# Storing every split weight tile, and loading the spectra's rows by two transfers of 64 partitions

## The chip, the cores and the metric

The kernel runs on one core of a Trainium2 chip. The metric is the device time of one execution in microseconds. The engines are TensorE (PE; its weight loads are listed apart as PEld), VectorE (DVE), ScalarE (ACT), GpSimd (POOL) and SyncE (SP), which issues most of the DMA transfers. A name with a q, such as SPq, is the queue of instructions by which an engine issues transfers. Each engine works through its own list of instructions in order, so that an instruction that waits holds up all that stand behind it on the same engine.

## The reference

The input `A_u` has 2048 positions of 448 values in float32. Three terms are added: the input, a state-space convolution and a gated block, the last two on the layer-normed input.

```python
x  = A_u                                   # (1, 2048, 448)
xn = layernorm(x)
# the convolution: a kernel of 2048 taps for each of 448 channels
P = exp((A * dt[:, None])[:, :, None] * pos)          # A = -exp(log_A_real) + i A_imag, 256 modes
K = 2 * einsum("dn,dnl->dl", C * dt, P).real
y = irfft(rfft(xn.T, 4096) * rfft(K, 4096))[:, :2048].T + xn * D_skip
# the gated block
h   = sigmoid(xn @ w_gate) * (xn @ w_up)              # (2048, 1792)
out = x + y + h @ w_down
```

`B_x` is not used: both blocks read the normed `A_u`.

## The kernel before, in words

The program is written as two generators, `conv()` and `glu()`, whose pieces are taken in turn according to how far each has come; a planner then places every instruction in its engine's order, with hints (`issue_after`, high priority) from the code. So TensorE's list alternates between matmuls of the gated block and of the convolution.

**The gated block (`glu`).** The 1792 columns of `w_gate` and `w_up` are cut into 14 tiles `f` of 128, in groups of 3, 3, 3, 3 and 2 (`GROUPS`). The positions are done in two halves. In each half every tile is used once: for each of two blocks of 512 positions `gate()` does two chains of eleven matmuls (`gu`, L711), one for each of the two matrices, then the activation and the product; after a group its part of `h @ w_down` is added up (`po`, L836). For precision each weight tile is split into a high part and the rest: `wh`, `wl` for gate and up (128 x 1024 float32 each, 512 KB), `dh`, `dl` for `w_down` (128 x 448, 224 KB each). `wh` and `wl` have two places, `dh` three and `dl` four.

In the first half a tile comes raw (`w_load` into `wraw`, one place; `rd_load` into `rd`), ScalarE makes the high part (L764, L796), VectorE the low part of `w` (L768) and GpSimd that of `d` (L797). The second half takes the groups in the order 2, 3, 4, 1, 0 (`ORDER`). For the nine tiles outside `RAW` the split parts were stored in DRAM in the first half (`wt_d`, `dt_d`, L787), and SyncE loads them (L780, L808). For the five tiles in `RAW`, which are 0, 1, 2, 4 and 5 and so nearly all of the last two groups, the raw tile is loaded a second time, one tile ahead (`coming`) or two (`coming_d`), and GpSimd splits it (L775, L776, L803, L804).

**The convolution (`conv`).** First the parameters are prepared (`prep`) and the first stage of the input's transform is done: 32 rows by 64 columns of positions, a matmul with the constant `wx`, rows stored in `x1_d` (128 rows, one for each real or imaginary part of a frequency in two halves of the columns). Then `kgen` makes the 2048 taps in 56 steps, on all engines, and `first_stage` does the same transform for them and stores rows in `sk_d`. This runs beside the gated block up to about 526 us.

Then `spectra` does the rest in 17 steps: for four frequencies `k` and one half `h` of the channels each (one step has the last frequency alone). `loads(h, k)` fetches the rows of `x1_d` into `sx` and of `sk_d` into `skl` (three places each; 448 KB each) and a table `tb`, three steps ahead; `there()` does the second stage of the transform on both (64 matmuls `pk` and `px`, L923) and evacuates them (ScalarE `oo`, VectorE L929 and L930); `product()` multiplies the spectra (VectorE L936 and L937, GpSimd L939 and L940); `halves()` follows on VectorE (L944, L945); one step later `back()` does the first stage of the inverse (32 matmuls L957 into the same PSUM tiles `pk` and `px`), ScalarE copies the result into `vt` (L963, two places), and SyncE stores it in `v_d` (L971 to L977). Every two steps `turned()` loads rows of `v_d` turned into `vp` (L983), for which SyncE waits until the store has landed. The last stage (`last`, L993) adds to the output.

In `loads` the 128 partitions of `sx` and of `skl` are filled by four transfers of 32 partitions each (`quarters`), since the four blocks of 32 rows lie in another order in DRAM: for `sk_d` the real and imaginary parts of a frequency stand 32 rows apart, and likewise for `x1_d`, where `wx` has 33 cosines first and then 31 sines.

Of the kernel before, what the change touches and what calls it, by code (L numbers as in the profile page):

```python
# [11 lines left out]
F32 = mybir.dt.float32  # L12
# [8 lines left out]
D = 448  # L21
# [23 lines left out]
FCH = [3, 3, 3, 3, 2]  # L45

GROUPS = [list(range(sum(FCH[:i]), sum(FCH[: i + 1]))) for i in range(len(FCH))]
RAW = set(GROUPS[0] + GROUPS[1][1:])
ORDER = [GROUPS, GROUPS[2:] + GROUPS[1::-1]]
DC = 8  # L50
LAG = 3
# [7 lines left out]
def _tables():  # L59

    a = np.arange(NA)[:, None]
    k1 = np.arange(NK1)[None, :]
    ang = 2 * np.pi * ((a * k1) % 64) / 64.0


    wk = np.zeros((4, NA, 2, 2, 32))

    wx = np.zeros((4, NA, 64))
    for j in range(4):
        wk[j, :, 0, j % 2] = np.cos(ang)[:, :32]  # L70
        wk[j, :, 1, j % 2] = -np.sin(ang)[:, :32]
        wk[j, :, 1, j % 2, 0] = np.cos(ang)[:, 32]
        wx[j, :, :NK1] = np.cos(ang)
        wx[j, :, NK1:] = -np.sin(ang)[:, 1:32]
    b = np.arange(NB)[:, None]
    k2 = np.arange(32)[None, :]
    rows = lambda t: t.reshape(32, 2, 32).transpose(1, 0, 2)
    tab = np.zeros((NK1, 2, 2, 32, 2, 32))
    bk = np.zeros((2, 32, 2, 2, 32, 2))
    for q in range(NK1):  # L80
        al = 2 * np.pi * ((b * (q + 64 * k2)) % 4096) / 4096.0
        c, s = rows(np.cos(al)), rows(np.sin(al))
        tab[q, :, 0, :, 0], tab[q, :, 0, :, 1] = c, -s
        tab[q, :, 1, :, 0], tab[q, :, 1, :, 1] = s, c
        if q in (0, 32):
            c, s = c.transpose(2, 0, 1), s.transpose(2, 0, 1)
            bk[q // 32, :, :, 0, :, 0], bk[q // 32, :, :, 0, :, 1] = c, s
            bk[q // 32, :, :, 1, :, 0], bk[q // 32, :, :, 1, :, 1] = -s, c

    tab[0, :, 1] = 0.0  # L90
    tab[32, :, 1] = tab[32, :, 0]
    tab[32, :, 0] = 0.0
    bk = np.tile(bk.reshape(2, 32, 256), (1, 4, 1))
    t32 = np.concatenate([tab[32].reshape(128, 64), bk[1]], 1)
# [34 lines left out]
def s4d_glu_kernel(ctx, tc, io):  # L129
# [326 lines left out]
    def kgen(pk):  # L456
# [127 lines left out]
        for g in range(NCK // NCH):  # L584
            for c in range(NCH):
# [42 lines left out]
                if cn % 4 == 3:  # L628
                    ks = tl["ks"]
                    nc.tensor.matmul(  # L630
                        ko[:, :, 0], ident, dm[:, cn // 4], start=False, stop=True, skip_group_check=True
                    )
                    nc.scalar.copy(ks.rearrange("p s (q b) -> p s q b", q=2), ko.rearrange("p s (b q) -> p s q b", q=2))
                yield WK / 3
                if cn % 4 == 2 and cn > 3 or cn + 1 == NCK:

# [26 lines left out]
    def kept(t, d, f):  # L663
        for i in range(2):
            flat = t[i].rearrange("p i k f -> p (i k f)") if len(t[i].shape) == 4 else t[i]
            yield flat.bitcast(F32), d[i, f]
# [63 lines left out]
        to.append((hh, hl))  # L730

    def glu():
        stores, later, coming, coming_d, rds = [], [], {}, {}, []
        last_fs = [f for fs_ in ORDER[1] for f in fs_]
        follow, second = dict(zip(last_fs, last_fs[1:])), dict(zip(last_fs, last_fs[2:]))
        for half in range(2):
            if half == 1:
                for q in (2, 3):
# [2 lines left out]
            for fs_ in ORDER[half]:  # L741
# [14 lines left out]
                for n_, (f, t) in enumerate(order):  # L756
                    if t == 0:
                        wh = pg.tile([128, 2, 4, 128], F32R, name="wh", bufs=2)
                        if half == 0:
# [8 lines left out]
                                    v.tensor_tensor(wl, raw, wh, ALU.subtract)  # L768
                            if not raws and f + 1 < NFT:
                                raws.append((w_load(f + 1), None))  # L770
                            if f not in RAW:
                                stores.extend(kept((wh, wl), wt_d, f))
                        elif f in RAW:
                            raw, wl = coming.pop(f), w_low()
                            nc.gpsimd.tensor_copy(wh, raw)  # L775
                            nc.gpsimd.tensor_tensor(wl, raw, wh, ALU.subtract)  # L776
                        else:
                            wl = w_low()
                            for t_, d_ in kept((wh, wl), wt_d, f):
                                nc.sync.dma_start(t_, d_)  # L780
                        if half == 1 and follow.get(f) in RAW:
                            coming[follow[f]] = w_load(follow[f])
                        ws.append((wh, wl))
                    between = (lambda s_=mid[n_]: step(*s_)) if cross and mid[n_] else None
                    yield from gate(ws[f - f0], xq[2 * half + t], hs[t], between)
# [4 lines left out]
                    if t == 0:  # L790
                        dh = pg.tile([128, D], F32R, name="dh", bufs=FCH[0])
                        if half == 0:
# [2 lines left out]
                            with hp(HP), tc.issue_after((act if f == 1 else marks)[0].ins):  # L795
                                nc.scalar.copy(dh, rd)  # L796
                            nc.gpsimd.tensor_tensor(dl, rd, dh, ALU.subtract)  # L797
                            if f not in RAW:
                                later.extend(kept((dh, dl), dt_d, f))
                        elif f in RAW:  # L800
                            dl = d_low()
                            rd = coming_d.pop(f)
                            nc.gpsimd.tensor_copy(dh, rd)  # L803
                            nc.gpsimd.tensor_tensor(dl, rd, dh, ALU.subtract)  # L804
                        else:
                            dl = d_low()
                            for t_, d_ in kept((dh, dl), dt_d, f):
                                nc.sync.dma_start(t_, d_)  # L808
                        if half == 1 and second.get(f) in RAW:
                            if len(rds) < 2:  # L810
                                tag, n = (("rdw", 1), ("rd", RB))[len(rds)]
                                rds.append(pg.tile([128, D], F32, name="rd", tag=tag, bufs=n))
                            else:
                                rds.append(rds.pop(0))
                            coming_d[second[f]] = rd_load(second[f], rds[-1])
                        wts.append((dh, dl))
                    yield 2.5
                    for s_ in end[n_] if cross else ():
# [41 lines left out]
    def spectra(pf):  # L860
# [8 lines left out]

        vp = {0: pf.tile([128, 32, H], F32, name="vp", bufs=1)}  # L870
        spare = {
            "vt": [pf.tile([128, 4, H], F32, name="vt", bufs=2)],
            "oo": [pf.tile([128, 2, H], F32, name="oo", bufs=2)],
            "kk": [pf.tile([128, 2, 2, H], F32, name="kk", bufs=1)],
        }
# [4 lines left out]
        def loads(h, k):  # L880
            sx = pf.tile([128, 4, H], F32, name="sx", bufs=NLD)
            sk = pf.tile([128, 7, 4, 32], F32, name="skl", bufs=NLD)
            turn_ = lambda r: slice(*{0: (0, 32), 32: (64, 96), 64: (32, 64), 96: (96, 128)}[r])
            quarters = [(32 * r, slice(32 * r, 32 * r + 32)) for r in (0, 2, 1, 3)]
            if k == 32:
                for r, s in quarters:
                    nc.sync.dma_start(sx[s, 0:2].rearrange("b h d -> b (h d)"), x1_d[r])
                for i in range(2):
                    for r, s in quarters:
                        nc.sync.dma_start(sk[s, :, i], sk_d[i, 0, turn_(r), :, :32])  # L890
                return None, sk, sx
            ds = slice(H * h, H * h + H)
            for r, s in quarters:
                nc.sync.dma_start(sx[s], x1_d[r + k : r + k + 4, :, ds].rearrange("k b d -> b k d"))
            if k not in tabs:
                tabs[k] = pf.tile([128, 4, 64], F32, name="tb", bufs=NTB)
                nc.sync.dma_start(tabs[k], io["c_tab"][k // 4])
            tb = tabs.pop(k) if h else tabs[k]

            for r, s in quarters:  # L900
                nc.sync.dma_start(sk[s].rearrange("p g k d -> p g (k d)"), sk_d[h, k // 4, turn_(r)])
            return tb, sk, sx

        def after():
# [41 lines left out]
            return sd  # L946

        def back(h, k, sd, engs=(nc.sync, nc.sync)):
            vt = work("vt", [128, 4, H], 2)
            n = 2 if k == 32 else 4  # L950
            bt = t32[:, 1:].rearrange("p (q e) m -> p q e m", q=2) if k == 32 else bk
            with after():
# [53 lines left out]
                out_end(ac[:, 4 * q - 8 : 4 * q - 4], 4 * q - 8, ds, [nc.sync])  # L1006

        ac = acl[0]
        lasts.append(last)
        nc.sync.dma_start(t32, io["c_t32"])  # L1010
        nc.gpsimd.dma_start(bk, io["c_bk"])
# [195 lines left out]
```

## The time and the profile before

| | us |
|---|---|
| median of three runs (745.04 to 748.52) | 745.27 |
| the profiled execution | 745.18 |
| its span, first to last instruction | 743.4 |
| TensorE busy | 666.0 (90%) |
| VectorE busy | 588.1 (79%) |
| ScalarE busy | 421.1 (57%) |
| GpSimd busy | 389.4 (52%) |
| mean granted TensorE clock | 0.955 |
| moved by DMA | 114.47 MB, 154 GB/s |

A busy share is a mean over stages that are limited by different things, so the stages have to be read apart. Rows of the profile give the line in the code (L711), the engine, the operation and the tiles, written as output<-input. In rows of a timeline the first number is the start, the second the duration; in brackets stands how long the engine had been idle before, and what ended that. Rows of waits read: who waited, for whom, total time, how many times, the longest. Rows by tile give the shortest, median and longest duration in ns. In windows the pairs are busy time and number of instructions; the last three columns are the granted clock, the share of time in which the 16 DMA engines were busy, and GB/s. The "chain" is the sequence of work that ended last, each piece with its duration.

### The profile page before, as it was taken

Reading aid. Unit: us, or ns where it says so; the run is one execution under the profiler, and the core shown is the slowest. Engines: PE = TensorE matmul, PEld = TensorE weight load, DVE = VectorE, ACT = ScalarE, POOL = GpSimd, SP = SyncE. Lnnn points to the kernel's source line nnn. Section 1 sums busy time; section 2 is a strip of 40 time slices with the busy share of each in tenths; the row PEclk is TensorE's granted clock in tenths of the full one; section 3 lists DMA queues with packets and bytes.
Section 4 is the critical chain, followed back from the end, with each engine's and each line's share of the span. In section 5 each row is a group of like instructions: output and inputs, shape, how many; then the busy total and the mean of one; then the engine's idle time right before and its main releaser. Section 6 shows DMA issues by size and latency. Waiting matters only on the chain.

```text
span 743.4 us, 20855 instructions
## 1 busy us (share of the span) xinstructions
PE 666.0 (90%) x8581; PEld 515.0 (69%) x8581; DVE 588.1 (79%) x779; ACT 421.1 (57%) x651; POOL 389.4 (52%) x415
## 2 busy tenths in 40 slices
PE   2898999998999998989999999999899888589895
PEld 1665788887877885558778878888666565356673
DVE  5799996798998998884789988879387865276753
ACT  3655572887788788973877787686223212122310
POOL 2120044987999887783357758674255433251301
PEclk9999999999999999988999999999999988779997
DMA  8935347355154553439522432331577577776355
GB/s 199 239 110 195 116 146 230 135 158 170 56 155 143 165 163 123 157 125 269 144 92 81 134 132 69 108 94 59 163 194 243 159 203 196 225 214 172 100 166 158
DMA packets 99311, 114.47 MB, mean 154 GB/s; under 512 B 13696, under 2 KB 90048, under 8 KB 98960
## 3 DMA queue, kind: packets, MB, share of 16 engines
q1 hardware_dynamic: 79664, 97.00, 44.3%
q10 hardware_dynamic: 18816, 14.57, 6.7%
q0 software_dynamic: 736, 1.56, 0.8%
q8 instruction: 68, 1.11, 0.6%
q14 instruction: 27, 0.22, 0.1%
HBM read 68.32 MB, written 44.76 MB: 152 GB/s over the span
## 4 chain that ended last, share of the span: by engine, by line
PE 33%; DVE 9%; DMA 8%; ACT 3%; issue 3%; SPq 3%; POOL 2%; ACTq 0%; DVEq 0%; POOLq 0%
PE gu L711 13%; PE po L836 6%; PE ko L620 3%; DMA skl<-sk_d 3%; DMA v_d<-vt 2%; DVE Ft L606 2%; PE tr L536 2%; PE pk L923 2%; DVE Et L604 1%; PE pk L957 1%; PE px L957 1%; PE kp L562 1%; DVE Et L605 1%; DMA acc_d<-acc 1%; PE px L923 1%
## 5 line engine op out<-in xcount | busy, mean ns | idle before, releaser
L514 POOL TENSOR_TENSOR me<-me,pm 128x32 f32<-128x32 f32 (+1 forms) x168 | 141.9, 845 | 91.5 <-DVE Et L605 78.3
L514 POOL TENSOR_TENSOR mf<-mf,pm 128x64 f32<-128x64 f32 (+1 forms) x112 | 119.2, 1064 | 6.0
L711 PE MATMUL gu<-xh,wh 128*128 128x512 f32 x336 | 103.4, 415 | 2.7 <-ACT xh L218 1.4
L711 PE MATMUL gu<-xh,wl 128*128 128x512 f32 x336 | 97.8, 398 | 0.0
L711 PE MATMUL gu<-xl,wh 128*128 128x512 f32 x336 | 96.5, 393 | 0.0
L605 DVE TENSOR_TENSOR Et<-me,S 128x1024 f32<-128x1024 f32 x56 | 80.3, 1434 | 12.1 <-ACT me L527 12.1
L606 DVE TENSOR_TENSOR Ft<-mf,S 128x1024 f32<-128x1024 f32 x56 | 83.2, 1485 | 8.0 <-PE ko L620 5.2
L836 PE MATMUL po<-dh,hh 128*128 128x448 f32 (+1 forms) x227 | 87.6, 386 | 1.2 <-ACT hh L727 0.9
L604 DVE TENSOR_TENSOR Et<-me,S 128x1024 f32<-128x1024 f32 x56 | 79.7, 1423 | 9.1 <-ACT S L547 8.9
L836 PE MATMUL po<-dl,hh 128*128 128x448 f32 (+1 forms) x227 | 85.1, 375 | 1.9 <-POOL dl L797 1.9
L836 PE MATMUL po<-dh,hl 128*128 128x448 f32 (+1 forms) x227 | 84.8, 374 | 2.1 <-DVE hl L729 2.1
L711 PEld LDWEIGHTS gu<-xh,wh 128*128 128x128 f32 x336 | 62.6, 194 | 24.7 <-issue 8.8
L727 ACT CAST hh<-gu 128x512 fp32r<-128x512 f32 x56 | 33.2, 593 | 81.9 <-DVE gu L722 80.0
L544 ACT ACTIVATE S<-tr 128x1024 f32<-128x1024 f32 x56 | 57.8, 1032 | 31.5 <-PE tr L536 29.8
L711 PEld LDWEIGHTS gu<-xh,wl 128*128 128x128 f32 x336 | 64.3, 192 | 15.6 <-issue 0.7
L711 PEld LDWEIGHTS gu<-xl,wh 128*128 128x128 f32 x336 | 63.8, 190 | 14.3 <-issue 0.7
L939 POOL TENSOR_TENSOR yy<-yy 128x448 f32<-128x448 f32 (+1 forms) x16 | 28.6, 1786 | 76.4 <-DVE yy L936 76.4
L620 PEld LDWEIGHTS ko<-Et,Ft 128*32 128x32 f32 x3584 | 53.4, 110 | 21.4 <-issue 10.5
L841 DVE SCALAR_TENSOR_TENSOR acc<-po,acc 128x448 f32<-128x448 f32 (+1 forms) x81 | 48.5, 609 | 23.1 <-PE po L836 23.0
L620 PE MATMUL ko<-Et,Ft 128*32 128x64 f32 x3584 | 63.1, 221 | 3.9 <-DVE Ft L606 3.9
L547 ACT ACTIVATE S<-S,hpi 128x1024 f32<-128x1024 f32 x56 | 65.7, 1173 | 0.0
L545 ACT ACTIVATE S<-tr 128x1024 f32<-128x1024 f32 x56 | 57.7, 1030 | 0.8 <-issue 0.8
(208 smaller groups left out, 1301.1 us busy)
## 6 DMA issues: line engine op xcount, KB each, us to landing
sk_d<-sk ACTq DMA_DIRECT2D x14, 512.0 KB
sx<-x_d SPq DMA_DIRECT2D x64, 112.0 KB
skl<-sk_d SPq DMA_DIRECT2D x64, 112.0 KB
vp<-v_d SPq DMA_DIRECT2D x8, 896.0 KB
v_d<-vt SPq DMA_DIRECT2D x27, 224.0 KB
wt_d<-wh SPq DMA_DIRECT2D x9, 512.0 KB
wt_d<-wl SPq DMA_DIRECT2D x9, 512.0 KB
wl<-wt_d SPq DMA_DIRECT2D x9, 512.0 KB
```

The source lines that it names most:

```text
L514: ins = nc.gpsimd.tensor_tensor(m[:, :, w + a : 2 * w : n], m[:, :, a:w:n], par(base + i).unsqueeze(2).to_broadcast([128, 4 * DC, w // n]) ...
L544: nc.scalar.activation(rows(cs), pv, AF.Abs)
L545: nc.scalar.activation(rows(S[:, 0:5:4]), pv, AF.Sin, scale=TWO_PI)
L547: sins[:] = [nc.scalar.activation(cs, cs, AF.Sin, scale=-TWO_PI, bias=hpi)]
L604: v.tensor_tensor(Et[:, :, :, 32:64], two(me[:, :, 32:64]), S[:, 1::-1], ALU.mult)
L605: v.tensor_tensor(Et[:, :, :, 0:32], two(me[:, :, 0:32]), S[:, 1:3, :, ::-1], ALU.mult)
L606: fts[:] = [v.tensor_tensor(Ft, two(mf), S[:, 3:5], ALU.mult)]
L620: nc.tensor.matmul(ko[32 * j : 32 * j + 32, sl], Ft[:, cc, DC * h + 4 * q + j], Et[:, cc, DC * h + 4 * q + j], start=(k == 0), stop=(k == ...
L711: glu_mm[:] = [nc.tensor.matmul(ps, a_, b_, start=(n == 0), stop=(n == len(mm) - 1))]
L727: nc.scalar.copy(hh, hf)
L836: glu_mm[:] = [nc.tensor.matmul(po[:, ds], a_[:, bs], w_[:, ds], start=(n == 0), stop=(n == 3 * fc - 1))]
L841: v.scalar_tensor_tensor(acc[:, b, ds], po[:, ds], 0.5, acc[:, b, ds], ALU.mult, ALU.add)
```

## The change

Three things change together.

1. `RAW` is gone: the split parts of all 14 tiles are stored in the first half and loaded in the second. The second loads of raw tiles (`coming`, `coming_d`, `rds`) and GpSimd's second splits (L775, L776, L803, L804) go.
2. The tables and one copy put the real and imaginary parts of a frequency in neighbouring rows (`wx`: cosines in even columns, sines in odd ones; `ks` is no longer reordered, so that the rows of `sk_d` come out interleaved). With that, `loads` fills `sx` and `skl` by two transfers of 64 partitions in place of four of 32.
3. `vt` gets a third place, in the memory of `wraw`, and the three are taken in turn.

```diff
-RAW = set(GROUPS[0] + GROUPS[1][1:])
...
-        wx[j, :, :NK1] = np.cos(ang)
-        wx[j, :, NK1:] = -np.sin(ang)[:, 1:32]
+        wx[j, :, 0::2] = np.cos(ang)[:, :32]
+        wx[j, :, 1::2] = -np.sin(ang)[:, :32]
+        wx[j, :, 1] = np.cos(ang)[:, 32]
...
-                    nc.scalar.copy(ks.rearrange("p s (q b) -> p s q b", q=2), ko.rearrange("p s (b q) -> p s q b", q=2))
+                    nc.scalar.copy(ks, ko)
...
-                            if f not in RAW:
-                                stores.extend(kept((wh, wl), wt_d, f))
-                        elif f in RAW:
-                            raw, wl = coming.pop(f), w_low()
-                            nc.gpsimd.tensor_copy(wh, raw)
-                            nc.gpsimd.tensor_tensor(wl, raw, wh, ALU.subtract)
+                            stores.extend(kept((wh, wl), wt_d, f))
                         else:
                             wl = w_low()
                             for t_, d_ in kept((wh, wl), wt_d, f):
                                 nc.sync.dma_start(t_, d_)
-                        if half == 1 and follow.get(f) in RAW:
-                            coming[follow[f]] = w_load(follow[f])
...
-                            if f not in RAW:
-                                later.extend(kept((dh, dl), dt_d, f))
-                        elif f in RAW:
-                            dl = d_low()
-                            rd = coming_d.pop(f)
-                            nc.gpsimd.tensor_copy(dh, rd)
-                            nc.gpsimd.tensor_tensor(dl, rd, dh, ALU.subtract)
+                            later.extend(kept((dh, dl), dt_d, f))
...
-            "vt": [pf.tile([128, 4, H], F32, name="vt", bufs=2)],
...
-            quarters = [(32 * r, slice(32 * r, 32 * r + 32)) for r in (0, 2, 1, 3)]
+            halves_ = [slice(64 * q, 64 * q + 64) for q in range(2)]
...
-            for r, s in quarters:
-                nc.sync.dma_start(sx[s], x1_d[r + k : r + k + 4, :, ds].rearrange("k b d -> b k d"))
+            for q, s in enumerate(halves_):
+                rows = x1_d[64 * q + 2 * k : 64 * q + 2 * k + 8, :, ds]
+                nc.sync.dma_start(sx[s], rows.rearrange("(k c) b d -> (c b) k d", c=2))
...
-            for r, s in quarters:
-                nc.sync.dma_start(sk[s].rearrange("p g k d -> p g (k d)"), sk_d[h, k // 4, turn_(r)])
+            for q, s in enumerate(halves_):
+                nc.sync.dma_start(sk[s].rearrange("p g k d -> p g (k d)"), sk_d[h, k // 4, q::2])
...
-            vt = work("vt", [128, 4, H], 2)
+            vts.append(vts.pop(0))
+            vt = vts[-1]
...
+        vts = [pf.tile([128, 4, H], F32, name="vt", bufs=2) for _ in range(2)]
+        vts.append(pg.tile([128, 4, H], F32, name="vt", tag="wraw", bufs=1))
```

More of the change, by code (lines that the diff above doesn't have):

```diff
@@ L732, in glu @@
     def glu():
-        stores, later, coming, coming_d, rds = [], [], {}, {}, []
-        last_fs = [f for fs_ in ORDER[1] for f in fs_]
-        follow, second = dict(zip(last_fs, last_fs[1:])), dict(zip(last_fs, last_fs[2:]))
+        stores, later = [], []
         for half in range(2):
@@ L808, in glu @@
                                 nc.sync.dma_start(t_, d_)
[L809 to L815, printed above, removed]
                         wts.append((dh, dl))
@@ L882, in loads @@
             sk = pf.tile([128, 7, 4, 32], F32, name="skl", bufs=NLD)
-            turn_ = lambda r: slice(*{0: (0, 32), 32: (64, 96), 64: (32, 64), 96: (96, 128)}[r])
-            quarters = [(32 * r, slice(32 * r, 32 * r + 32)) for r in (0, 2, 1, 3)]
+            halves_ = [slice(64 * q, 64 * q + 64) for q in range(2)]
             if k == 32:
-                for r, s in quarters:
-                    nc.sync.dma_start(sx[s, 0:2].rearrange("b h d -> b (h d)"), x1_d[r])
+                for q, s in enumerate(halves_):
+                    to = sx[s, 0:2].rearrange("b h d -> b (h d)")
+                    nc.sync.dma_start(to, x1_d[64 * q : 64 * q + 2].rearrange("c b d -> (c b) d"))
                 for i in range(2):
-                    for r, s in quarters:
-                        nc.sync.dma_start(sk[s, :, i], sk_d[i, 0, turn_(r), :, :32])
+                    for q, s in enumerate(halves_):
+                        nc.sync.dma_start(sk[s, :, i], sk_d[i, 0, q::2, :, :32])
                 return None, sk, sx
             ds = slice(H * h, H * h + H)
-            for r, s in quarters:
-                nc.sync.dma_start(sx[s], x1_d[r + k : r + k + 4, :, ds].rearrange("k b d -> b k d"))
+            for q, s in enumerate(halves_):
+                rows = x1_d[64 * q + 2 * k : 64 * q + 2 * k + 8, :, ds]
+                nc.sync.dma_start(sx[s], rows.rearrange("(k c) b d -> (c b) k d", c=2))
             if k not in tabs:
@@ L898, in loads @@
             tb = tabs.pop(k) if h else tabs[k]
-            for r, s in quarters:
-                nc.sync.dma_start(sk[s].rearrange("p g k d -> p g (k d)"), sk_d[h, k // 4, turn_(r)])
+            for q, s in enumerate(halves_):
+                nc.sync.dma_start(sk[s].rearrange("p g k d -> p g (k d)"), sk_d[h, k // 4, q::2])
             return tb, sk, sx
```

## The prediction

> **What bounds the kernel now.** I read the page's slices first, then busy time by stretches, then TensorE's waits in the worst stretch, then the queue or engine behind each wait. The slices (about 18.6 us each) show the granted TensorE clock, the share of the DMA engines and the bytes per time:
>
> ```profile
> PEclk9999999999999999988999999999999988779997
> DMA  8935347355154553439522432331577577776355
> GB/s 199 239 110 195 116 146 230 135 158 170 56 155 143 165 163 123 157 125 269 144 92 81 134 132 69 108 94 59 163 194 243 159 203 196 225 214 172 100 166 158
> ```
>
> The clock sags at the end, where DMA is steadily at 0.7. The stretches, with each engine's busy time, clock, DMA share and GB/s:
>
> ```profile
> core 0 of [0], span 743.4 us
> core 0: us, PE busy (x) PEld busy (x) DVE busy (x) ACT busy (x) POOL busy (x), PEclk, DMA share, GB/s
> 0.00:60.00 60.00, 43.84 (x206) 31.62 (x210) 48.01 (x112) 28.46 (x44) 10.59 (x25) 0.97 0.76 189
> 350.00:526.00 176.00, 172.44 (x2773) 142.45 (x2772) 148.39 (x154) 131.77 (x188) 113.36 (x133) 1.00 0.34 103
> 566.00:665.00 99.00, 75.27 (x1025) 53.88 (x1017) 62.07 (x88) 21.71 (x43) 41.70 (x31) 0.84 0.74 212
> 665.00:685.00 20.00, 19.58 (x270) 13.89 (x255) 13.94 (x22) 4.89 (x9) 5.43 (x4) 1.00 0.64 167
> 685.00:713.00 28.00, 24.82 (x365) 17.17 (x363) 21.47 (x34) 8.45 (x17) 6.24 (x4) 0.88 0.35 100
> ```
>
> From 350 to 526 TensorE is the bound: 172.4 of 176 us busy, clock 1.00. From 566 to 665, where the spectral steps meet the last split weights, it stands 99.0 - 75.3 = 23.7 us, and what it does runs at 0.84. If the slow clock falls on busy and idle time alike, its work at full clock is 75.3 x 0.84 = 63.2 us (estimate), so 12.0 us are slow clock: 99 = 63.2 + 12.0 + 23.7. This stage is what the change is worth. Its waits on TensorE (total, times, longest):
>
> ```profile
> PE pk L957 <- DVE kk L930: 13.4, 4, 10.5
> PE pk L923 <- ACT vt L963: 6.6, 3, 2.9
> PE pk L923 <- DMA skl<-sk_d: 3.6, 1, 3.6
> ```
>
> **The change part by part.**
>
> *No weight is split twice.* Out go, for tiles 0, 1, 2, 4, 5 in the second half, a raw load into `wraw`/`rd` and four GpSimd instructions. GpSimd's time is worth nothing by itself (41.7 of 99 us busy), but its order is. The long wait, on GpSimd's timeline:
>
> ```profile
> 623.26 2.04 POOL L939 TENSOR_TENSOR yy<-yy 128x448 f32<-128x448 f32 x1 [2.10 <-DVE yy L936]
> 642.59 0.56 POOL L803 CAST dh<-rd 128x448 fp32r<-128x448 f32 x1 [17.29 <-DMA rd<-in_B_w_down_dram]
> 643.11 1.12 POOL L940 TENSOR_TENSOR yy<-xx 128x448 f32<-128x448 f32 x1
> 644.19 1.13 POOL L804 TENSOR_TENSOR dl<-rd,dh 128x448 fp32r<-128x448 f32 x1
> ```
>
> L940 of a spectral step stands 17.3 us behind a cast for the last `po` group, which waits for a late `rd`. VectorE's L944 waits for L940, everything on VectorE stands behind it, and L957 waits 10.5 us. Without the cast L940 follows L939 at 625.3. What is late next is VectorE's ordinary evacuation, which costs in a calm step:
>
> ```profile
> 688.41 0.99 PE L957 MATMUL pk<-xx,bk 32*64 32x224 f32 x16 [1.22 <-DVE kk L930]
> ```
>
> So 10.5 becomes 1.2: **-9.3**.
>
> *The third place for `vt`.* The 6.6 us are the next step's matmuls waiting for PSUM, whose copy into `vt` waits for the store of two steps before:
>
> ```profile
> ACT vt L963 <- DMA v_d<-vt: 24.9, 5, 7.6
> ```
>
> With three places the copy looks at a store one step (some 10 us) older, more than the longest of these waits, 7.6. **-6.6**. The third place has no user left by then (by the diff `wraw` is loaded in the first half only, and `x1`, which shares it, is stored with the first half's last group).
>
> *Transfers of 64 partitions.* SyncE's queue over two steps of the stage:
>
> ```profile
> 588.41 1.30 SPq L977 DMA_DIRECT2D v_d<-vt  x2
> 592.32 0.50 SPq L983 DMA_DIRECT2D vp<-v_d  x1
> 592.92 1.95 SPq L901 DMA_DIRECT2D skl<-sk_d  x4
> 594.98 2.89 SPq L894 DMA_DIRECT2D sx<-x_d  x4
> 599.01 1.24 SPq L977 DMA_DIRECT2D v_d<-vt  x2
> 600.35 2.42 SPq L901 DMA_DIRECT2D skl<-sk_d  x4
> 602.87 1.79 SPq L894 DMA_DIRECT2D sx<-x_d  x4
> 604.76 0.39 SPq L646 DMA_DIRECT2D wraw<-in_B_w_gate_dram  x1
> 605.20 1.80 SPq L648 DMA_DIRECT2D wraw<-in_B_w_gate_dram  x2
> 607.04 0.59 SPq L646 DMA_DIRECT2D wraw<-in_B_w_up_dram  x1
> 607.67 1.13 SPq L648 DMA_DIRECT2D wraw<-in_B_w_up_dram  x2
> 608.91 0.62 SPq L977 DMA_DIRECT2D v_d<-vt  x1
> ```
>
> It is never free: 20.5 us a round (588.41 to 608.91), against 63.2/99 x 20.5 = 13.1 us of TensorE's work. So loads go out late. Afterwards: `v_d` 1.30, the wait for its landing 2.6, `vp` 0.5, two `skl` 1.0, two `sx` 1.2 (bound from above by two `v_d` stores, also 64 partitions of four short rows), a wait as before 599.01 of 1.1, `v_d` 1.24, `skl` 1.0, `sx` 1.2, and in place of 4.1 us of raw loads two issues like this one:
>
> ```profile
> L780 SPq DMA_DIRECT2D wh<-wt_d x9: 337/338/387, 298.2 to 493.0; - x9
> ```
>
> Together 11.9 us, below 13.1. If 64 partitions take as long to issue as two of 32, only the raw loads go: 20.5 - 3.4 = 17.1. The 3.6 us wait for `skl` goes in the first case and stays in the second, and its landing is unchanged either way; I take half: **-1.8**.
>
> *The clock.* Idle left is 23.7 - 9.3 - 6.6 - 1.8 = 6.0. Short gaps cost clock too: in 685 to 713, 3.2 us idle go with 24.8 x 0.12 = 3.0 us of slow clock, about one for one. The gate of eleven matmuls behind the 1.22 us gap above, and a later one, in the chain:
>
> ```profile
> 690.46 4.31 PE gu L711 x11
> ...
> 696.44 2.72 PE gu L711 x11
> ```
>
> So 6.0 of the 12.0 stays: **-6.0** (ends: 0, and -9.0 if the loss shrinks in proportion to the idle time). [...]
>
> *More bytes.* In this stage two raw `w` loads of 736 KB become pairs of 1024 KB and one `rd` load of 224 KB becomes up to three pairs of 448 KB: +1.7 MB on 212 x 99 = 21.0 MB. What is left by the terms so far is 99 - 23.7 = 75.3 us. If the DMA engines were never free they would need 22.7 MB / (212/0.74 = 286 GB/s) = 79.4 us, and at the best slice's 269 GB/s 84.4. So 4 to 9 us come back; output and `ac` transfers may slip past 665, where the share is 0.64 and 0.35, so I stay near the lower end: **+5.0**.
>
> *Five more tiles stored in the first half*, 4 issues and 1472 KB each, on SyncE, the `dt` pair behind GpSimd's `dl`:
>
> ```profile
> SPq L787 <- POOL dl L797: 38.9, 8, 8.5
> ```
>
> Five more such waits would be 5 x 4.9 = 24 us of SyncE's time, with `ph` and the next raw tile queued behind; TensorE is covered by a raw tile's lead over its gate. Where the lead is thin is the start: tiles 0 and 1 add 3.0 MB to the first 60 us, 12 us of the DMA engines at 189/0.76 = 249 GB/s, and 0.24 x 60 = 14.4 us are free. Bounds 0 (bytes are only added, so no gain) and 12; the nearest wait is ACT's for a raw tile:
>
> ```profile
> 53.22 1.05 ACT L764 CAST wh<-wraw 128x1024 fp32r<-128x1024 f32 x1 [1.49 <-DMA wraw<-in_B_w_up_dram]
> ```
>
> I take **+1.5**.
>
> *At nothing:* the `ks` copy moves the same 512 elements per partition, fourteen times; TensorE's work up to 526 hides it, and even 1 us more of each would cost at most 14 us bare. The tables are constants. After 665 the last stores and loads keep their lengths: 0, plus or minus 2.
>
> **Sum:** -9.3 - 6.6 - 1.8 - 6.0 + 5.0 + 1.5 = -17.2. The profiled execution took 745.18 (1.8 around its span), 0.1 below the median: 745.2 - 17.2 = **728.0**.
>
> **The rivals.**
>
> *All of it comes back.* Transfers slip freely past 665, the first stage absorbs its stores, `skl` is never late, the clock loss shrinks in proportion: -9.3 - 6.6 - 3.6 - 9.0 = -28.5, 716.7. For it: the DMA share of 0.35 after 685. Against: the share of 0.74 before.
>
> *Only GpSimd's stall goes.* `v_d`'s landing, not the place, holds the steps: -9.3, clock in proportion 12.0 x 9.3/23.7 = -4.7, +5.0 + 1.5: 737.7. For it: SyncE's own order, store, landing, `vp`, `skl`, stays serial.
>
> *The transfers set the pace, no change.* If the best slice wholly inside the stage, 225 GB/s, is what rows this short give, 22.7 MB take 100.9 us against 99 now: 745.2 + 1.9 + 1.5 = 748.6 at most, 746 if some slip past 665. For it, one load's landing, three times the issue of its four parts:
>
> ```profile
> 592.92 6.02 DMA skl<-sk_d
> ```
>
> [...] Against the rival: 269 GB/s in one slice.
>
> *Slower: SyncE stands behind a weight load.* The split pair goes straight into `wh`/`wl`, so SyncE must wait until the gates of the tile two before are over; raw loads waited for `wraw` only. Now:
>
> ```profile
> SPq L780 <- PE gu L711: 10.2, 9, 4.0
> ```
>
> That was harmless while SyncE had little else. Here `sx` and `skl` stand behind. A stop ordered before loads that TensorE needs next costs issue and landing, 1.0 + 6.0, and clock at 12.0/23.7 of it, 3.5: 10.5 us. Four tiles load here; four stops: +42 - 23.7 + 1.5 = 765. Against: each load has a whole tile of gates as lead. It decides from the second stop on (17.2/10.5 = 1.6).
>
> **How the numbers follow.** Forecast 0.45, all of it 0.17, only the stall 0.14, transfers 0.13, slower 0.11. A measurement can tell about 0.5%, 3.7 us, from no change. Faster: 0.45 + 0.17 + 0.14 = 0.76; same 0.13; slower 0.11. The range 713 to 745 takes in the first three and a part of the fourth, and leaves out the slower case, the rest of the fourth and a tail below.
>
> **What would show it.** Right: no L775, L776, L803, L804 on GpSimd; the 10.5 us wait at L957 and ACT's waits for `v_d` gone; steps (L923 to L923) of about 8 us instead of some 10 between 566 and 665; SyncE idle at times there; a DMA share near 0.9; clock above 0.9. Wrong: TensorE waiting for `skl` or `sx` with a weight load just ahead on SyncE, or an order of the planner's that shifts work in the first half.

## The result, and the profile after

| | before | after |
|---|---|---|
| median of eight runs each, us | 746.14 | 741.62 (738.91 to 743.78) |
| ratio, with its 95% interval | | 0.9933 [0.9907, 0.9959] |
| span of the profiled execution, us | 743.4 | 742.0 |
| moved by DMA, MB | 114.47 | 125.76 |
| GpSimd busy, us | 389.4 | 350.7 |

The change gains 4.5 us where 17.2 were forecast. 741.6 lies inside the range, near its upper end. The slices of the page of the changed kernel, 18.6 us each, to be held against those of before:

```profile
PEclk9899999999999899787899999999999899969989
DMA  8986558444244453433854243233389987889356
GB/s 202 261 264 248 172 178 275 152 158 149 74 126 166 140 134 102 151 121 109 244 144 138 64 132 95 75 113 95 110 199 294 255 242 205 256 215 284 113 154 171
```

In slices 33 to 36 (595 to 668 us) the clock read 8, 8, 7, 7; now it reads 9, 9, 9, 6, with DMA at 8, 7, 8, 8 where it was at 7 in all four. But in slices 17 to 20 (297 to 371 us), where it read 9, 8, 8, 9, a deeper sag stands now: 7, 8, 7, 8. The windows of the changed kernel (columns as in the prediction):

```profile
0.00:60.00 60.00, 41.59 (x185) 30.43 (x186) 46.21 (x109) 27.43 (x43) 10.49 (x25) 0.94 0.91 245
60.00:170.00 110.00, 106.69 (x735) 85.23 (x734) 99.58 (x146) 68.14 (x109) 50.58 (x58) 0.98 0.59 194
170.00:290.00 120.00, 113.46 (x1725) 92.58 (x1724) 109.54 (x113) 93.86 (x135) 96.98 (x98) 0.96 0.39 123
290.00:350.00 60.00, 52.20 (x678) 31.19 (x676) 44.49 (x55) 46.87 (x77) 32.16 (x44) 0.83 0.39 123
350.00:526.00 176.00, 174.30 (x2650) 143.08 (x2651) 144.88 (x152) 128.73 (x186) 108.94 (x133) 0.98 0.42 127
566.00:665.00 99.00, 81.25 (x1184) 58.08 (x1184) 70.43 (x104) 26.72 (x51) 32.78 (x22) 0.89 0.89 246
```

and the same stretches of the kernel before that the prediction did not show:

```profile
60.00:170.00 110.00, 104.06 (x727) 84.34 (x723) 99.39 (x149) 71.87 (x115) 53.07 (x59) 1.00 0.51 162
170.00:290.00 120.00, 115.50 (x1862) 92.93 (x1864) 111.86 (x117) 97.39 (x143) 105.66 (x103) 0.99 0.43 130
290.00:350.00 60.00, 53.93 (x711) 36.85 (x706) 46.39 (x57) 42.45 (x69) 36.83 (x46) 0.91 0.61 189
```

Between 566 and 665 us TensorE does 1184 matmuls in place of 1025: the stage gains. From 170 to 526 us it does fewer, 5053 against 5346, at a lower clock: something is lost there, where the change was thought to touch nothing. Where it is lost is seen when the start of the same `po` group of the gated block is compared in the two traces. In the changed kernel it stands later by 2.9 us at 114 us (time of the kernel before), 9.5 at 241, 13.5 at 312, 14.6 at 461; then it catches up: later by 6.2 at 612, earlier by 0.1 at 723. So **14.6 us are lost before the spectral steps and 14.7 are won back in them**.

The stage looks as forecast in most points. A spectral step (start of `pk` to the next) takes 8.2 us (ten steps, 561.64 to 643.98) where it took 10.2 (seven, 565.50 to 636.72), each up to the longest wait of the stage. TensorE's waits in it, changed kernel:

```profile
PE pk L972 <- DMA vp<-v_d: 9.9, 1, 9.9
PE pk L936 <- DVE kk L908: 3.6, 3, 1.3
PE gu L711 <- DMA wh<-wt_d: 3.0, 1, 3.0
PE pk L901 <- ACT vt L942: 1.0, 2, 0.5
```

The 10.5 us behind GpSimd are gone (L936 is the old L957; 1.3 is the longest now), and TensorE's wait for `vt` falls from 6.6 to 1.0. ScalarE's own waits for `v_d`, which were to go, fall from 24.9 to 6.2 us. But a wait of 9.9 us for `vp` is new. SyncE's list there, and the end of the wait on TensorE:

```profile
643.90 1.67 SPq L956 DMA_DIRECT2D v_d<-vt  x2
646.23 1.13 SPq L879 DMA_DIRECT2D skl<-sk_d  x2
647.46 1.26 SPq L872 DMA_DIRECT2D sx<-x_d  x2
648.76 0.61 SPq L875 DMA_DIRECT2D tb<-in_c_tab_dram  x1
649.47 1.25 SPq L956 DMA_DIRECT2D v_d<-vt  x2
655.76 0.50 SPq L962 DMA_DIRECT2D vp<-v_d  x1
661.65 1.78 PE L972 MATMUL pk<-vp,wf 64*32 64x224 f32 x32 [9.89 <-DMA vp<-v_d]
```

The load of `vp` waits for the store issued at 649.47, and both stand in line on SyncE: the copy for that store was over at 634.28, 15.2 us ahead of it. Here the third place let ScalarE copy earlier, but the store waited for its turn on SyncE.

What is slow in the middle shows on TensorE itself. The same operations, first in the changed kernel, then in the kernel before:

```profile
298.94 1.50 PE L283 MATMUL gu<-xt,wx 32*64 32x448 f32 x4 [1.48 <-DVE xr L222]
300.47 1.93 PE L620 MATMUL ko<-Et,Ft 128*32 128x64 f32 x64
302.33 1.22 PE L536 MATMUL tr<-sel,ph 128*128 128x512 f32 x2
305.17 1.65 PE L711 MATMUL gu<-xh,wh 128*128 128x512 f32 x3
```

```profile
300.63 0.97 PE L283 MATMUL gu<-xt,wx 32*64 32x448 f32 x4
301.86 1.10 PE L620 MATMUL ko<-Et,Ft 128*32 128x64 f32 x64
303.14 0.71 PE L536 MATMUL tr<-sel,ph 128*128 128x512 f32 x2
306.28 0.93 PE L711 MATMUL gu<-xh,wh 128*128 128x512 f32 x3 [1.11 <-DVE xr L222]
```

The changed kernel takes 1.93 us where 1.10 was enough, for some 10 us on end, and 1.48 us is the longest wait in the 40 us ahead of it. So the loss is largely slow clock: counted as the prediction did, length times (1 - clock) over the five stretches up to 526 us, it is 24.3 us after and 8.4 before, 15.9 more, about the 14.3 by which the `po` group at 515 us is late.

### The profile page after: what moved, and what is told of

It reads as the page before. It is cut to its first block, busy times and chain, and to the rows that moved or that the text cites. A ratio compares the mean times of both kernels' runs of the same rounds, so it can differ in the third digit from the quotient of the medians.

```text
span 742.0 us, 20710 instructions
## 1 busy us (share of the span) xinstructions
PE 671.6 (91%) x8581; PEld 515.9 (70%) x8581; DVE 584.2 (79%) x779; ACT 421.6 (57%) x651; POOL 350.7 (47%) x395
## 2 busy tenths in 40 slices
DMA packets 97630, 125.76 MB, mean 169 GB/s; under 512 B 12656, under 2 KB 85808, under 8 KB 97280
## 4 chain that ended last, share of the span: by engine, by line
PE 54%; DVE 14%; DMA 10%; ACT 6%; POOL 6%; issue 5%; SPq 3%; ACTq 0%; DVEq 0%; POOLq 0%
PE gu L711 20%; PE po L814 15%; PE ko L620 5%; PE tr L536 3%; POOL me L514 3%; DVE Ft L606 3%; DVE Et L605 2%; DVE Et L604 2%; PE gu L283 2%; PE pk L936 2%; DMA vp<-v_d 2%; POOL mf L514 2%; DMA wh<-wt_d 1%; PE pk L901 1%; DMA v_d<-vt 1%
## 5 line engine op out<-in xcount | busy, mean ns | idle before, releaser
L514 POOL TENSOR_TENSOR me<-me,pm 128x32 f32<-128x32 f32 (+1 forms) x168 | 134.4, 800 | 107.0 <-DVE Et L605 94.7
L711 PE MATMUL gu<-xh,wh 128*128 128x512 f32 x336 | 105.8, 422 | 7.5 <-ACT xh L218 4.5
L605 DVE TENSOR_TENSOR Et<-me,S 128x1024 f32<-128x1024 f32 x56 | 74.9, 1337 | 20.0 <-ACT me L527 15.7
L604 DVE TENSOR_TENSOR Et<-me,S 128x1024 f32<-128x1024 f32 x56 | 79.8, 1424 | 9.5 <-ACT S L547 9.5
L544 ACT ACTIVATE S<-tr 128x1024 f32<-128x1024 f32 x56 | 57.9, 1034 | 30.3 <-PE tr L536 23.7
L620 PEld LDWEIGHTS ko<-Et,Ft 128*32 128x32 f32 x3584 | 55.1, 113 | 24.1 <-issue 9.7
L620 PE MATMUL ko<-Et,Ft 128*32 128x64 f32 x3584 | 64.7, 225 | 5.9 <-DVE Ft L606 5.6
L719 ACT ACTIVATE th<-gu 128x512 f32<-128x512 f32 x56 | 34.0, 607 | 43.4 <-PE gu L711 43.4
```

Of the source, the lines that this page charges most:

```text
L514: ins = nc.gpsimd.tensor_tensor(m[:, :, w + a : 2 * w : n], m[:, :, a:w:n], par(base + i).unsqueeze(2).to_broadcast([128, 4 * DC, w // n]) ...
L544: nc.scalar.activation(rows(cs), pv, AF.Abs)
L604: v.tensor_tensor(Et[:, :, :, 32:64], two(me[:, :, 32:64]), S[:, 1::-1], ALU.mult)
L605: v.tensor_tensor(Et[:, :, :, 0:32], two(me[:, :, 0:32]), S[:, 1:3, :, ::-1], ALU.mult)
L620: nc.tensor.matmul(ko[32 * j : 32 * j + 32, sl], Ft[:, cc, DC * h + 4 * q + j], Et[:, cc, DC * h + 4 * q + j], start=(k == 0), stop=(k == ...
L711: glu_mm[:] = [nc.tensor.matmul(ps, a_, b_, start=(n == 0), stop=(n == len(mm) - 1))]
```

## The experiments

The planner writes TensorE's list. Of its 5345 instructions 866 stand at another place in the changed kernel than before, all from the 476th to the 2993rd: the middle of the run. Leaving parts of the change out shows which part does that: the two stores of `dh` and `dl` of **tile 5 alone**. Without them 18 instructions differ. So theory A: the new order costs the 11 to 14 us. Theory B: the traffic of the five added tiles costs them. Theory C: another part of the change does.

### The stores of single tiles

**no5**, **no012** and **nostore** don't store tile 5, tiles 0 to 2, or all five, and so compute another output; **bstore** is the kernel before that stores all 14 but loads as before. Core of the edits (`nostore` has all five tiles in the list; the second half then loads other tiles' parts):

```diff
-                            stores.extend(kept((wh, wl), wt_d, f))
+                            if f not in (5,):
+                                stores.extend(kept((wh, wl), wt_d, f))
```

> The changed kernel without the stores of tile 5 (the second half reads tile 10's parts in its place, so the output is another). Without these four stores the planner puts TensorE's list up to 526 us back to that of the kernel before in all but 18 of 5345 places. Theory A (the planner's order of the first half costs about 11 of the 14 us that the changed kernel lies behind at the start of the spectra): 731, lag against the kernel before about 3 us at 350 us of the span. Theory B (the stores' traffic costs it): only a fifth of the traffic goes, 739, lag still 12.

> The changed kernel without the stores of tiles 0, 1 and 2 (the second half reads tiles 6, 7, 8 in their place, so the output is another); TensorE's list is that of the changed kernel in every place. Theory A (order): only what the first 60 us lose comes back, 3.5 us: 738. Theory B (traffic): three fifths of the stored bytes and all of them in the crowded start go, 8 to 11 us come back: 731 to 734.

> The changed kernel without the stores of tiles 0, 1, 2, 4 and 5 (the second half reads tiles 6 to 10 in their place, so the output is another); TensorE's list is that of the kernel before in all but 18 places. Theories A and B alike: the lag before the spectra goes, 728. If instead the tables, the plain copy of ks or the new second half cost the first half its time (theory C): about 741.

> The kernel before with all 14 tiles stored and nothing else changed; TensorE's list up to the end is that of the changed kernel. Theories A and B: the kernel before plus 14 us less what its own stall hides, 757 to 760. Theory C (the stores and the order they bring cost nothing, the lag comes from the rest of the change): 746.

Then the smallest part, and two versions of the whole change that keep the old order nearly: **no5d** leaves out the two `dt` stores of tile 5, and so computes another output; **d5pool** issues these two from GpSimd's queue (65 instructions from the order before); **d5late** issues tile 5's four stores two gates later (215).

```diff
-                            later.extend(kept((dh, dl), dt_d, f))
+                            later.extend((t_, d_, nc.gpsimd if f in (5,) else nc.sync) for t_, d_ in kept((dh, dl), dt_d, f))
```

> The changed kernel without the two 224 KB stores of tile 5's dh and dl (the second half reads tile 10's in their place, so the output is another); all other stores are there. The planner's TensorE list goes back to that of the kernel before but for 18 places. Theory A (order): 728, as without all of tile 5's stores; lag against the kernel before under 3 us at 460 us of the span. Theory B (traffic): half a megabyte in 742 us of transfers, no change, 741.

> The changed kernel, complete, with those same two stores issued by GpSimd instead of SyncE. The bytes are all there; TensorE's list differs from that of the kernel before in 65 of 5345 places, from the changed kernel's in 897. Theory A: 728 to 731. If the two stores cost time by being made at all: 741.

> The changed kernel, complete, with all four stores of tile 5 issued by SyncE two gates later. TensorE's list differs from that of the kernel before in 215 places, from the changed kernel's in 830. Theory A, if what counts is being near the old list: 728 to 733. If any departure from the old list costs, or the stores themselves: 738 to 742.

### The three parts apart

The second question is which part gains in the spectra. **vt2**, **quart** and **part1** are the changed kernel without the third place, with four transfers of 32 partitions, and with both (stored tiles alone); all three have the changed kernel's order on TensorE. **halves** is the kernel before with two transfers of 64 alone, and its order.

```diff
-        vts.append(pg.tile([128, 4, H], F32, name="vt", tag="wraw", bufs=1))
```

> The changed kernel without the third place for vt (everything else as in it; TensorE's list of instructions is the changed kernel's). Theory F (the prediction's term): the matmuls' wait for the copy into vt comes back, 6.6 us, and with it its share of the clock's term, 6.0 x 6.6/17.7 = 2.2: 741.6 + 8.8 = 750.4, and the trace shows ACT waiting for v_d<-vt again in the spectral steps. Theory G (SyncE's order holds the steps: v_d's store is issued some 15 us after the copy into vt, so that a place one step older is not what is late): within 2 us of the changed kernel, 740 to 744.

> The changed kernel with x and kernels loaded by four transfers of 32 partitions, with the tables and the copy into ks of the kernel before (TensorE's list is the changed kernel's). Theory F (the prediction's term): the wait for skl comes back, 1.8 us taken, 3.6 whole, with 0.6 to 1.2 of clock: 744 to 746.4. Theory G (SyncE's queue still sets the pace of the spectral steps in the changed kernel): a round of it grows by the prediction's 17.1 - 11.9 = 5.2 us, over the three or four steps in which TensorE waits behind it: +15 to +21, 757 to 763, with longer waits for vp, sx or skl on TensorE between 566 and 665 us.

> The changed kernel's stored tiles alone: x and kernels by four transfers of 32 partitions and two places for vt, as in the kernel before (TensorE's list is the changed kernel's). Theory F: the sum of the two terms, 741.6 + 8.8 + 2.4 = 753, of which the first half's loss of 14.5 stays and the spectra gain GpSimd's 9.3 less what the bytes take back. Theory G: as with quarters alone, 757 to 763, the place for vt adding nothing.

> The kernel before with x and kernels loaded by two transfers of 64 partitions, with their tables and the copy into ks; nothing else (TensorE's list is that of the kernel before). Theory F: -1.8 (0 to -3.6) and some clock: 0.994 to 1.0 of the kernel before, about 743.5 beside 745.2. Theory G (SyncE's queue sets the pace): a round of 20.5 us loses 2.0 + 1.6 or so of issue in each of six steps, but the raw loads and GpSimd's 10.5 us stay, so that between a third and all of it shows: -6 to -18, ratio 0.976 to 0.992.

The same three edits on **d5pool**, whose middle is calm:

> The changed kernel with tile 5's two dt stores issued by GpSimd, and without the third place for vt. Theory F (the prediction's term): 726.3 + 6.6 + 2.2 = 735. Theory G (SyncE's queue was what made v_d's stores late; with halves the place is not the limit): within 3 us of d5pool, 723 to 729, ratio to the kernel before 0.970 to 0.977.

> The changed kernel with tile 5's two dt stores issued by GpSimd, and x and kernels by four transfers of 32 partitions as before. Theory F: 726.3 + 2 to 5 = 728 to 731. Theory G: as much as the changed kernel lost by it, 750.05 - 741.6 = 8.4, to the 13 that halves alone gave: 735 to 739, with TensorE waiting for skl or vp in the spectra.

> The changed kernel with tile 5's two dt stores issued by GpSimd, but with four transfers of 32 partitions and two places for vt: stored tiles alone, in the calm order. Theory F: GpSimd's 9.3 and its clock less what the bytes take back: 745.2 - 9.3 - 4.7 + 5.0 = 736. Theory G: what stored tiles alone gained in the spectra in the disturbed order, 7.4, or a little less, since SyncE's queue takes the rest: 737 to 741, and within 3 us of d5_quart (the third place adds nothing there either).

### All results

"Middle" is how much later or earlier the `po` group at 461 us stands than the one at 114, each against the kernel before; "spectra" the same from 461 to 723; both from the profiled execution. The ratios are to runs of the kernel before that were timed beside each kernel, whose medians lie between 744.6 and 746.8 us.

| kernel | TensorE's order | median, us | ratio to before, 95% interval | middle | spectra |
|---|---|---|---|---|---|
| after | new | 741.6 | 0.9933 [0.9907, 0.9959] | +11.7 | -14.7 |
| bstore | new | 761.1 | 1.0189 [1.0141, 1.0238] | +15.5 | -1.8 |
| no012 | new | 738.4 | 0.9897 [0.9844, 0.9949] | +10.1 | -14.9 |
| vt2 | new | 737.8 | 0.9888 [0.9845, 0.9930] | +8.9 | -15.5 |
| quart | new | 750.1 | 1.0049 [1.0019, 1.0079] | +9.0 | -9.2 |
| part1 | new | 750.2 | 1.0057 [1.0025, 1.0088] | +10.8 | -7.4 |
| no5 | old but for 18 | 728.3 | 0.9738 [0.9682, 0.9795] | -1.6 | -15.9 |
| no5d | old but for 18 | 729.1 | 0.9750 [0.9725, 0.9776] | -3.5 | -16.4 |
| nostore | old but for 18 | 726.4 | 0.9724 [0.9678, 0.9770] | -2.8 | -15.9 |
| halves | old | 731.8 | 0.9797 [0.9754, 0.9840] | -1.6 | -13.0 |
| d5late | old but for 215 | 729.0 | 0.9751 [0.9727, 0.9775] | -2.2 | -16.4 |
| d5pool | old but for 65 | 726.3 | 0.9727 [0.9694, 0.9761] | +0.4 | -18.6 |
| d5_vt2 | old but for 65 | 727.3 | 0.9750 [0.9700, 0.9801] | -1.8 | -16.3 |
| d5_quart | old but for 65 | 742.3 | 0.9960 [0.9928, 0.9991] | -3.1 | -1.9 |
| d5_part1 | old but for 65 | 737.7 | 0.9865 [0.9806, 0.9924] | -1.0 | -5.6 |

**The order.** Six kernels with the new order lose 8.9 to 15.5 us in the middle, nine with the old one between -3.5 and +0.4, whatever else they hold. Theory A holds. B falls with d5pool and d5late, which store every byte the changed kernel stores and lose nothing, and with no5d, where 448 KB left out are worth 12.5 us. C falls with bstore, which loses without parts 2 and 3; it stands 1 us above the 757 to 760 expected. The lists of VectorE, ScalarE and GpSimd move together with TensorE's, so it is the planner's order as a whole that is shown to cost, not TensorE's list alone.

One rival is left by the runs: all six kernels with the new order have the two stores of tile 5 at one and the same place of SyncE's list, and none of the nine has, so a hold-up of SyncE by them could be the cause. The windows between the two `po` groups (114 and 461 us) decide it; in order, the kernel before, the changed kernel, bstore, d5late and d5pool:

```profile
113.79:461.09 347.30, 332.48 (x4711) 264.32 (x4710) 298.74 (x332) 265.74 (x393) 255.17 (x286) 0.98 0.46 143
116.68:475.67 358.99, 342.69 (x4711) 268.87 (x4710) 299.96 (x332) 265.58 (x393) 244.85 (x286) 0.95 0.44 137
116.34:479.08 362.74, 344.07 (x4710) 269.93 (x4709) 299.20 (x332) 265.66 (x393) 244.39 (x287) 0.94 0.44 138
115.10:460.20 345.10, 332.82 (x4710) 263.91 (x4709) 299.34 (x332) 266.57 (x393) 265.82 (x286) 0.98 0.45 143
116.32:464.01 347.69, 336.04 (x4710) 266.26 (x4709) 299.16 (x333) 265.83 (x393) 257.58 (x289) 0.97 0.45 142
```

Where SyncE's queue was late in the spectra, TensorE stood in a wait (9.9 us for `vp`); in this stretch its idle time grows only from 14.8 to 16.3 us in the changed kernel (to 18.7 in bstore, which is 15.5 us late). The same 4711 matmuls take 10.2 us longer, at a clock of 0.95 for 0.98. In all six kernels the clock of this stretch is 0.94 or 0.95 and TensorE's busy time 8.6 to 11.6 us longer than in the kernel before; in the nine it is 0.97 to 0.99. d5pool fits too, though it has 0.84 from 290 to 350 us: its matmuls take 3.6 us longer, and its idle time is 3.2 us shorter. So the loss goes through the clock. Why the new order lowers it stays open, since no run changes the clock alone.

**The first 60 us.** no012 was expected to show a cost of the early stores. Its `po` group at 58 us is on time, and after's is 3.5 us late; but vt2, with all the stores, is 0.2 late, and halves, with none added, 2.5. So what differs there comes and goes without the stores, and a cost of theirs can't be told from it.

**Halves.** Two transfers of 64 partitions do most of the work, alone: 0.9797. What the window of the stage shows, two rows of its waits on TensorE, and one of GpSimd's timeline:

```profile
566.00:665.00 99.00, 80.08 (x1201) 56.98 (x1200) 69.39 (x102) 24.70 (x48) 45.14 (x32) 0.91 0.83 212
```

```profile
PE pk L959 <- DVE kk L932: 16.0, 3, 13.5
PE pk L925 <- ACT vt L965: 1.3, 1, 1.3
632.27 0.56 POOL L804 CAST dh<-rd 128x448 fp32r<-128x448 f32 x1 [15.09 <-DMA rd<-in_B_w_down_dram]
```

GpSimd's stall is there still, 13.5 us long, and the third place is not; yet the wait for `vt` has gone from 6.6 to 1.3 and the stage does 1201 matmuls for 1025. The joined transfers did not move bytes with less: 212 GB/s at a DMA share of 0.83, where it was 212 at 0.74. SyncE's waits from 545 to 700 us, before and then in halves, say why: it now waits for the copy into `vt` 7 times for 2, which means that its stores go out as soon as there is something to store.

```profile
SPq L977 <- ACT vt L963: 8.0, 2, 7.5
```

```profile
SPq L979 <- ACT vt L965: 19.9, 7, 7.5
```

The issue itself, by tile, in the kernel before and in the changed kernel, in ns (shortest, median, longest):

```profile
L894 SPq DMA_DIRECT2D sx<-x_d x64: 302/430/1217, 526.4 to 674.8; - x64
L901 SPq DMA_DIRECT2D skl<-sk_d x64: 303/421/1747, 528.7 to 672.9; - x64
```

```profile
L872 SPq DMA_DIRECT2D sx<-x_d x32: 594/600/636, 538.7 to 678.9; - x32
L879 SPq DMA_DIRECT2D skl<-sk_d x32: 445/544/1184, 540.7 to 677.0; - x32
```

Four times 0.430 against two times 0.600, and 4 x 0.421 against 2 x 0.544, are 0.52 + 0.60 = 1.12 us a step, and 16 steps make 17.9 us of SyncE's time (by medians). Halves gained 15. In the other pairs the two transfers are worth 8 to 16 us: quart to after 8.4, part1 to vt2 12.5, d5_part1 to d5_vt2 10.4, d5_quart to d5pool 16.0. Theory G holds for them: SyncE's queue set the pace of the stage. Its sizes were right for halves (15 of 6 to 18) and too large for quart (8.4 of 15 to 21) and part1 (750.2 of 757 to 763); d5_quart lost more than 8.4 to 13, and stands 4.6 from d5_part1 where at most 3 was expected; vt2 stands 2 us below its 740 to 744.

**The third place** is worth nothing in any pair: vt2 to after +3.9, d5_vt2 to d5pool -1.1, part1 to quart -0.2, d5_part1 to d5_quart +4.6; the intervals of the first three pairs overlap, and in the last it rather costs. With two places the waits for `vt` are there again (vt2, 566 to 665 us, the changed kernel without the third place):

```profile
ACT vt L942 <- DMA v_d<-vt: 24.9, 5, 8.8
PE pk L901 <- ACT vt L942: 10.1, 2, 9.0
```

and TensorE has no wait for `vp`. With three places, in the changed kernel, TensorE waits 1.0 us for `vt` and 9.9 for `vp`: the lateness has moved. In quart, 566 to 665 us, three places with four transfers, TensorE has no such wait for `vt` and these two:

```profile
PE pk L970 <- DMA vp<-v_d: 5.8, 1, 5.8
PE pk L899 <- DMA skl<-sk_d: 5.1, 3, 3.6
```

**Stored tiles** alone gain 7.4 us in the spectra (part1) and 5.6 (d5_part1, 0.9865). On top of halves they add little: 731.8 to 727.3 (d5_vt2), with overlapping intervals.

### The stores of `v_d` from ScalarE

If SyncE's queue is the bound, less in it should gain more. **actvd** is d5pool with all stores of `v_d` issued by ScalarE, which makes `vt`:

```diff
-        def back(h, k, sd, engs=(nc.sync, nc.sync)):
+        def back(h, k, sd, engs=(nc.scalar, nc.scalar)):
```

> As the kernel with tile 5's two stores on GpSimd, and besides all stores of v_d issued by ScalarE, which makes vt. TensorE's list is the same. Theory D (SyncE's list still holds the spectra: the last store of the first half of the channels goes out 15 us after its copy, and TensorE waits 9.9 us for vp): the wait falls under 2 us and some slow clock goes with it, 12 us less than with the stores on SyncE, 716 to 718. Theory E (the transfers are the limit, DMA share 0.95 around that wait): the store goes out earlier but lands no sooner, under 3 us less, 726 to 729.

It takes 741.31 us, 0.9925 [0.9898, 0.9952], 15 more than d5pool. Theory D fails, and E too. ScalarE's timeline, and the waits of the stage:

```profile
606.27 8.02 ACTq L954 DMA_DIRECT2D v_d<-vt  x4
614.34 0.53 ACT L905 COPY oo<-pk 128x448 f32<-128x448 f32 x1 [8.10 <-DMA v_d<-vt]
```

```profile
PE pk L936 <- DVE kk L908: 26.2, 5, 11.2
ACT oo L905 <- DMA ac<-acc_d: 13.5, 1, 13.5
```

ScalarE's copies `oo` stand in the same list behind its stores. The four at 606.27 went out over 8.02 us. Their issues took 0.58 to 0.60 us each, 2.4 in all; what held ScalarE between them the trace doesn't name. The 13.5 us of `oo` end at 567.5, behind the first store of `v_d`, which went out at 564.6 though its copy was over at 554.0; the profile puts that wait down to a load of `ac` that SyncE issued. VectorE waits for `oo`, TensorE for VectorE. The queue was relieved, and the engine loaded whose copies TensorE needs.

## Why the prediction was right or wrong

- **Five more tiles stored in the first half, +1.5: wrong; the step that failed.** The changed kernel is 14.6 us late before the spectral steps. The bounds of 0 to 12 were for traffic and waits at the start. What happened was the last thing named among those that could make it wrong, an order of the planner's that shifts work in the first half, and it had no price and no chance. It is some 11 us (8.9 to 15.5 in six kernels), and it comes in by two transfers of 224 KB, through a lower clock and not through waits.
- **The sum of the stage, -9.3 - 6.6 - 1.8 - 6.0 + 5.0 = -18.7: near.** -14.7 in the changed kernel, -16.4 and -18.6 in the two complete kernels with a calm middle (d5late, d5pool). These take 729.0 and 726.3 us, and the forecast was 728.0. That is luck in good part, for the terms are not what the sum was made of:
- **Transfers of 64, -1.8: mis-sized.** 8 to 16 us. Only the wait that carries the name `skl` was put down to them. SyncE's queue was seen to be full, 20.5 us a round against 13.1 us of work; the waits behind it carry the names of whatever stood in it, `vt` among them.
- **Third place, -6.6: wrong.** 0. The wait was real, but the place wasn't late; the store was. With a third place the lateness turns up as 9.9 us at `vp`. The rival that only GpSimd's stall goes held this of `v_d`'s landing, with "SyncE's own order" as its ground.
- **GpSimd's stall, -9.3: the wait went, the gain didn't follow it.** In halves a stall of 13.5 us stands and the kernel gains 15; stored tiles alone gain 5.6 to 7.4 in the spectra, and some 4 on top of halves. How much of that is the stall and how much the raw loads' issues is not separated.
- **The clock, -6.0: half of it.** 0.89 where "above 0.9" was written. By the prediction's reckoning slow clock falls from 12.0 to 81.25 x 0.11 = 8.9 us, 3.1 less.
- **The bytes, +5.0: not measured apart.** DMA is at 0.89, where "near 0.9" was written. The bytes were counted low: a raw `w` load is 512 KB (two transfers of 192 KB and four of 32), not 736, and the window moves 246 x 99 = 24.4 MB, 3.4 more than before where 1.7 were counted.
- **Slower, SyncE behind a weight load:** one wait of TensorE for `wh`, 3.0 us; not the four stops of that rival.
- **Transfers set the pace:** the window moves 246 GB/s, where that rival allowed 225.

On the clock, 1.93 us stand for 1.10 at 300 us, where it fell to 0.50 behind gaps of at most 1.48 us (0.73, 0.61 and 1.48 in the 7 us ahead of it). The next fall, at 330 us, to 0.50 as well, comes behind a gap of 4.07 us. What brings a fall was not shown.

## What to carry to other kernels

When one queue issues everything, price an edit by the issue time it takes out of that queue over all steps (here 1.12 us a step, 16 steps: 17.9 us, of which 8 to 16 showed), not by the wait that carries the tile's name: the buffer added here behind a full queue only moved the wait, from 10.1 us at `vt` (vt2) to 9.9 at `vp`. Where a planner writes the order, a small new instruction can reorder a stretch far from the stage it serves: compare the start of the same groups in both traces before any theory on bandwidth, and move the instruction to another queue or place before giving the change up. Here the whole change with two stores moved takes 726.3 us in place of 741.6.

## What the runs showed of the hardware

- TensorE's clock fell to 0.50 with no gap over 1.48 us on the engine, which had been busy for 37.18 of the 40 us ahead. In the changed kernel, before and after the fall:

```profile
259.00:299.00 40.00, 37.18 (x642) 29.38 (x641) 35.55 (x40) 31.31 (x47) 28.40 (x35) 1.00 0.41 113
299.20:309.40 10.20, 10.17 (x84) 5.84 (x81) 6.05 (x7) 8.40 (x15) 6.33 (x12) 0.50 0.38 120
330.43 1.76 PE L283 MATMUL gu<-xt,wx 32*64 32x448 f32 x4 [4.07 <-DVE xl L216]
```

  The third row stands at the next fall, behind a gap of 4.07 us; from 330.4 to 340 us the clock was 0.50.
- An issue on SyncE took a median of 0.600 us for 64 partitions of `sx` and 0.430 for 32, and 0.544 and 0.421 for `skl`: joining two saved about a third of the queue's time.
- An issue of `v_d` took as long on ScalarE's queue (0.58 to 0.60 us in the four above) as on SyncE's (0.57 to 0.60 in the four below). But the four went out over 8.02 us on ScalarE's in actvd and over 3.31 on SyncE's in the changed kernel, and what stood behind them in the list waited as long (8.10 us for `oo` in actvd):

```profile
623.19 3.31 SPq L954 DMA_DIRECT2D v_d<-vt  x4
```
